# Attention and two expert layers on one core: engines of the moves chosen by a table, transposed probabilities in single banks, last keys of a pair in one operation

## The chip, the cores and the metric

The kernel runs on one core of a Trainium2 chip. The metric is the device time of one execution in microseconds (us). The core has five engines with a queue each: PE (TensorE, the matrix unit; its weight loads are shown apart as PEld), DVE (VectorE), ACT (ScalarE), POOL (GpSimd) and SP (SyncE, which here only starts transfers). SBUF is the memory that all of them work in; PSUM is the small memory of eight banks into which PE writes.

## The reference, cut to what matters

```python
def reference(q, k, v, moe, moe2):            # q, k, v: batch 2, 8 heads, 576 tokens, 64 columns
    q_rot, k_rot = rotate(q), rotate(k)       # x1*cos - x2*sin, x1*sin + x2*cos
    s = q_rot @ k_rot.T / 8
    p = exp(s - s.max(-1))
    p = p / (p.sum(-1) + 1e-09)
    x = (p @ v)                               # 1152 tokens x 512
    h = x @ moe.w_in                          # 512 x 2048
    x = (h * tanh(softplus(h))) @ moe.w_out   # 2048 x 512
    h = x @ moe2.w_in
    P = a[0] + a[1] * h + a[2] * h**2 + a[3] * h**3
    Q = 1.0 + abs(b[0]) * abs(h) + abs(b[1]) * h**2
    return (P / (Q + 1e-6)) @ moe2.w_out
```

All products are fp32. The kernel splits each factor into a high part that the fast product type takes and a low remainder, and adds three products: high by high, high by low, low by high. The four weight matrices arrive as 64-bit numbers, and their conversion to a high and a low part is work for ACT and DVE.

## The kernel before

**Stages.** The eight pairs of heads (four of batch 0, then four of batch 1) are the attention stage. The two expert layers follow, m = 0 (line 1034's `Mish`) and m = 1 (the `ratio` function), each in 12 steps: four chunks of 512 hidden columns by three blocks of 384 tokens. A step has two `up` operations of 24 products (L1012) and, a step later, three or four `down` operations of 12 products (L1096), whose sums are collected by `down.add` (L1100 copies the first chunk, L1102 adds the others).

**One pair of attention.** `turned` rotates q and k (`rope.1` to `rope.4`, L620 to L624; for the first keys L594 to L602). `columns` transposes them on PE (L643); ACT moves the high part out of PSUM (`turn.hi`, L658) and DVE the low part (`turn.lo`, L662). Scores come in five tiles (`score`, L719); the last 64 keys of a row are taken apart from the first 512 in `rests` (L690 on PE, `rest.move` L695 on ACT, `rest.max` L697 on DVE), once for tiles 0 and 1 and once for tiles 2 and 3. DVE scales a tile and takes its maximum (`score.max`, L734 and L754), ACT takes the exponential and its sum (`score.exp`, L738 and L759). `turn_p` transposes the probabilities (L786 to L796) into two neighbouring banks at a time, which are taken and given back together; `p.move` copies them to SBUF (L811), on ACT and DVE by turns. `weigh` multiplies by v (L845), and `weigh.move` copies the result (L850, ACT). `shares` turns the sums into factors: DVE adds 1e-9 and inverts (L865, L866, through a PSUM bank), PE transposes and spreads (L870, L878, L880), DVE scales (`x.scale`, L885), POOL splits into high and low (`x.hi` L896, `x.lo` L898).

**What sets the order.** Nothing in the program runs in the order in which it is written. `Plan.op` records every operation with an engine, an assumed cost, and what it reads and writes. `Plan.emit` then walks through time: it takes again and again the operation that could start first by these assumed costs, after a waiting penalty from the table `YIELD`, and breaks ties by a rank that the table `EARLY_LATE` shifts. It also hands out the PSUM banks. Operations named in `SHARED` (rotations, splits and the like, with their operands in SBUF) are not allowed to overlap one another in this walk, on whichever of DVE and POOL they are. The result is a fixed sequence for each engine; on the chip an engine does its sequence in order, and waits where an operand or a bank is not ready.

Of the kernel before, what the change touches and what calls it, by code (L numbers as in the profile page):

```python
# [44 lines left out]
def pool(n, wide=False):  # L45
# [13 lines left out]
    "down": -2293, "down.0": 1013, "down.add": -6295, "down.add.0": 4566, "g.hi": -9315, "g.hi.0": -1569, "g.lo":  # L59
# [51 lines left out]
YIELD = {  # L111
# [37 lines left out]
class Plan:  # L149
# [3 lines left out]
    def __init__(self):  # L153
# [56 lines left out]
    def emit(self, banks=8):  # L210
# [57 lines left out]
        while len(issued) < n:  # L268
# [24 lines left out]
            if names[i].removesuffix(".0") in SHARED:  # L293
                shared = end
# [902 lines left out]
```

## Time and profile before

| what | value |
|---|---|
| median of 3 runs | 539.42 us (539.36 to 539.58) |
| the profiled execution | 539.58 us, of which 537.7 us from its first to its last instruction |
| busy over the span | PE 97%, DVE 84%, ACT 68%, POOL 18% |
| granted TensorE clock | 1.00, which is the level of 2.4 GHz |
| first score, end of the last attention product, last expert product | 9.14 us, 139.45 us, 533.7 us |

A busy PE is not a PE at its best pace, since the ends of products are modelled and overlap. Whether it lost time is therefore read from the distance between the starts of two groups of products, compared with the same group elsewhere.

### The profile page before, as it was taken

How to read it: one execution, taken by the hardware profiler on the slowest of the kernel's cores; microseconds unless marked ns; L12 is line 12 of the kernel's file. 1: busy time of each engine (PE TensorE's matmuls, PEld its weight loads, DVE VectorE, ACT ScalarE, POOL GpSimd, SP SyncE). 2: the span in 40 equal slices, each digit the busy share in tenths (PEclk: the TensorE clock that was granted, in tenths of full speed). 3: DMA queues.
4: the chain of work that ended last, by engine and by line, in shares of the span. 5: the costliest groups of instructions: out<-in, count | busy, mean ns of one | idle time of the engine just before them, and what ended most of it. 6: DMA issues, size and time to landing. Idle time of an engine off the chain costs nothing.

```text
span 537.7 us, 9631 instructions
## 1 busy us (share of the span) xinstructions
PE 523.7 (97%) x3784; PEld 476.6 (89%) x3784; DVE 453.1 (84%) x704; ACT 367.5 (68%) x562; POOL 96.5 (18%) x100
## 2 busy tenths in 40 slices
PE   4999999999999999999999999999999999999997
PEld 3777777777999999999999999999889999889985
DVE  5789899998688959979788776999999898988892
ACT  3888889898786638697486667557677555676540
POOL 6899999212100000000000000000000000000000
PEclk9999999999999999999999999999999999999999
DMA  5433420033819494657639421044017003000022
GB/s 136 110 86 113 92 61 24 23 102 103 299 80 400 195 333 157 269 203 285 263 145 362 194 93 67 1 157 157 0 35 279 2 0 132 25 1 0 1 78 99
DMA packets 38684, 69.40 MB, mean 129 GB/s; under 512 B 22000, under 2 KB 24560, under 8 KB 37104
## 3 DMA queue, kind: packets, MB, share of 16 engines
q1 hardware_dynamic: 37824, 68.50, 35.5%
q8 instruction: 30, 0.49, 0.4%
q10 hardware_dynamic: 816, 0.30, 0.2%
q14 instruction: 14, 0.11, 0.1%
HBM read 53.84 MB, written 14.94 MB: 128 GB/s over the span
## 4 chain that ended last, share of the span: by engine, by line
PE 92%; ACT 4%; DVE 2%; issue 1%; DMA 0%; SPq 0%; DVEq 0%; ACTq 0%
PE banks L1012 37%; PE banks L1096 37%; PE banks L845 6%; PE banks L719 5%; PE banks L796 3%; PE banks L690 2%; ACT f L738 1%; ACT f L759 1%; PE banks L878 1%; PE banks L643 1%; ACT x L811 1%; DMA x<-in_k 0%; DVE f L594 0%; DVE x L811 0%; DVE f L754 0%
## 5 line engine op out<-in xcount | busy, mean ns | idle before, releaser
L1012 PE MATMUL banks<-r 128*128 128x384 f32 x1152 | 203.9, 335 | 0.0
L1096 PE MATMUL banks<-r 128*128 128x384 f32 (+1 forms) x1008 | 201.8, 358 | 0.0
L1012 PEld LDWEIGHTS banks<-r 128*128 128x128 f32 x1152 | 200.3, 188 | 0.9
L1096 PEld LDWEIGHTS banks<-r 128*128 128x128 f32 x1008 | 180.9, 188 | 16.4
L1022 ACT CAST r<-f 128x768 fp32r<-128x768 f32 x24 | 20.0, 833 | 40.8 <-DVE f L1070 40.8
L759 ACT ACTIVATE f<-f 128x576 f32<-128x576 f32 x56 | 43.1, 773 | 3.8 <-DVE f L754 3.7
L1034 ACT ACTIVATE r<-banks 128x768 fp32r<-128x768 f32 x24 | 19.6, 815 | 37.7 <-PE banks L1012 37.7
L845 PE MATMUL banks<-x,f 128*64 128x256 f32 (+1 forms) x320 | 42.4, 410 | 0.2
L719 PE MATMUL banks<-r 64*128 64x512 f32 (+2 forms) x264 | 39.9, 395 | 1.1 <-ACT r L658 0.5
L754 DVE TENSOR_SCALAR_CACHE_REDUCE f<-banks,f 128x512 f32<-128x512 f32 x56 | 38.8, 746 | 1.0
L1054 ACT ACTIVATE f<-banks 128x768 f32<-128x768 f32 x24 | 19.5, 812 | 25.9 <-PE banks L1012 25.9
L845 PEld LDWEIGHTS banks<-x,f 128*64 128x64 f32 x320 | 22.6, 136 | 14.8 <-DVE f L754 1.6
L1038 DVE TENSOR_TENSOR r<-f,r 128x768 fp32r<-128x768 f32 x24 | 22.8, 956 | 14.4 <-ACT f L1034 14.4
L1102 DVE TENSOR_TENSOR x<-banks,x 128x384 f32<-128x384 f32 (+1 forms) x42 | 25.0, 609 | 11.3 <-PE banks L1096 11.2
L1062 DVE TENSOR_TENSOR f<-f,banks 128x768 f32<-128x768 f32 x24 | 22.9, 953 | 13.2 <-ACT f L1060 13.0
L418 ACT ACT_TABLE_LOAD x26 | 33.4, 1283 | 0.5
L719 PEld LDWEIGHTS banks<-r 64*128 64x128 f32 (+1 forms) x264 | 27.7, 204 | 4.6 <-DVE r L662 0.8
L811 DVE COPY x<-banks 128x512 f32<-128x512 f32 (+2 forms) x52 | 28.4, 571 | 3.1 <-PE banks L796 2.0
L796 PEld LDWEIGHTS banks<-f 64*128 64x128 f32 x576 | 22.3, 141 | 5.6 <-ACT f L759 1.8
L811 ACT COPY x<-banks 128x512 f32<-128x512 f32 (+2 forms) x52 | 24.2, 495 | 4.3 <-PE banks L796 3.7
L796 PE MATMUL banks<-f 64*128 64x64 f32 x576 | 25.6, 230 | 0.8 <-DVE r L662 0.4
L1023 DVE TENSOR_TENSOR r<-f,r 128x768 fp32r<-128x768 f32 x24 | 22.9, 956 | 3.2 <-ACT r L1022 2.8
(95 smaller groups left out, 735.7 us busy)
## 6 DMA issues: line engine op xcount, KB each, us to landing
f<-in_moe_w_in SPq DMA_DIRECT2D x16, 1024.0 KB, 5.7
f<-in_moe_w_out SPq DMA_DIRECT2D x16, 1024.0 KB, 5.7
outside<-f SPq DMA_DIRECT2D x12, 1024.0 KB, 5.0
r<-outside SPq DMA_DIRECT2D x12, 1024.0 KB, 6.0
x<-in_k SPq DMA_DIRECT2D x15, 128.0 KB, 3.0
out<-x SPq DMA_DIRECT2D x5, 256.0 KB, 2.3
f<-in_q SPq DMA_DIRECT2D x8, 128.0 KB, 2.9
f<-in_v SPq DMA_DIRECT2D x8, 128.0 KB, 2.1
```

Of the source, the lines that this page charges most:

```text
L418: nc.scalar.preload_act_table_set(name)
L719: nc.tensor.matmul(o, qT[r, x, t * 128:(t + 1) * 128], kT[r, y, hf * w:(hf + 1) * w], start=(n == 0), stop=(n == 2))
L754: nc.vector.tensor_scalar(x[:, 0:8], bank(P).rearrange("p (k j) -> p k j", j=64), -0.125, nr, ALU.mult, ALU.min, accum_out=nm)
L759: nc.scalar.activation(view(at, 9, 64), x, AF.Exp, bias=nm, scale=-1.0, accum_out=sm)
L796: nc.tensor.transpose(bank(P)[:, hf, (i + n) * 64:(i + n + 1) * 64], x[r, f:f + 128], idf[r, r])
L811: (nc.scalar.copy if engine == "ACT" else nc.vector.tensor_copy)(o, i)
L845: nc.tensor.matmul(bank(P)[64 * a:64 * a + 64, 0:n], l, r, start=(kb == 0), stop=(kb == 4), skip_group_check=True)
L1012: nc.tensor.matmul(bank(P)[:, i, 0:BW], y[:, cb, f], x[:, cb, tok], start=(cb == 0 and n == 0), stop=(cb == CB - 1 and n == 2))
L1023: plan.op("g.lo", "DVE", dve(N), lambda: nc.vector.tensor_tensor(gl, g, gh.bitcast(F32), ALU.subtract), r=[(x,), (dst, u, "h")], w=[(dst, ...
L1062: plan.op("ratio.5", "DVE", dve(N, True), lambda: nc.vector.tensor_tensor(t, t, h(), ALU.mult), r=[(P,), (ba,)], w=[(bt,)])
L1096: nc.tensor.matmul(bank(P)[:, 0:n], x, y, start=(f == 0 and j == 0), stop=(f == FT - 1 and j == 2))
L1102: nc.vector.tensor_tensor(total(), bank(P)[:, 0:n], total(), ALU.add)
```

## The change

1. **A letter table.** `Plan.op` takes alternatives (`other`): the same work on another engine with another cost. A new table `ENGINES` says for each recorded operation which it is (A, D or P for ACT, DVE or POOL). It is open to `p.move`, `turn.hi`, `weigh.move`, `sum.row`, `rest.move` and the first `down.add` (ACT or DVE), the rotations, `x.lo`, `w.bound`, `w.lo` and `g.low` (POOL or DVE), and `x.hi` (POOL or ACT).
2. **Single banks.** The transposed probabilities of a full tile go into two banks that are taken and given back one by one.
3. **Last keys once.** `rests` does all four tiles of a pair in one product group of 24, one move of 512 columns and one maximum. The grid in SBUF has a tenth row for it.
4. **Sums.** ACT adds the 1e-9, and DVE inverts from SBUF to SBUF, so no bank is held for it.
5. **New tables.** `EARLY_LATE` and `YIELD` are new throughout, and so the whole sequence is another one.

```diff
 EARLY_LATE = {
-    "down": -2293, "down.0": 1013, "down.add": -6295, "down.add.0": 4566, "g.hi": -9315, "g.hi.0": -1569, "g.lo":
+    "down": 5156, "down.0": -6929, "down.add": -17362, "down.add.0": -2506, "down.add.0.ACT": 8843, "down.add.ACT":
...
+ENGINES = {
+    "down.add": "AAAADDDDDDDDDDDDDDDDDDDDDDDDDDDDDDDDDDDDDDDDDDAADDDADDDDDDDDDDDDDDDDDDDDDDDDD", "down.add.0":
+    "DADA", "g.low": "DPDDDDDDDPPPPPDPDDDDDP", "g.low.0": "PP", "p.move@0": "DADAAAAAAAA", "p.move@1":
...
-    def op(self, name, engine, cost, fn, r=(), w=(), late=0.0, after=(), form=None):
+    def op(self, name, engine, cost, fn, r=(), w=(), late=0.0, after=(), form=None, other=()):
         i = len(self.ops)
+        ways = [(engine, name, cost, fn)] + [(e, f"{name}.{e}", c, f) for e, c, f in other]
+        letter = ENGINES.get(name + at, "")[n:n + 1]
+        way = next((x for x in ways if x[0][0] == letter), ways[0])
+        engine, mark, cost, fn = way
...
-                    if names[i].removesuffix(".0") in SHARED:
+                    if names[i].removesuffix(".0") in SHARED and ops[i][0] in ("DVE", "POOL"):
                         t = max(t, shared)
...
-            for i in range(2):
-                t = 2 * u + i
+            for t in range(4):
                 for n, (x, y) in enumerate(((0, 0), (0, 1), (1, 0))):
                     for h, r in enumerate(HALVES):
-                        nc.tensor.matmul(bank(P)[:, h, i * 64:(i + 1) * 64], qT[r, x, t * 128:(t + 1) * 128],
+                        nc.tensor.matmul(bank(P)[:, h, t * 64:(t + 1) * 64], qT[r, x, t * 128:(t + 1) * 128],
                                          kT[r, y, 512:S], start=(n == 0), stop=(n == 2))
...
-        P = Banks(2)
+        P = [Banks(1), Banks(1)] if what == "m" and t < 4 else [Banks(2)]
...
-            T["moves"] = T.get("moves", 0) + 1
-            if T["moves"] % 2:
-                plan.op("p.move", "ACT", act(n), lambda hf=hf: move("ACT", hf), r=[(P,)], w=w)
-            else:
-                plan.op("p.move2", "DVE", dve(n, True) + (0 if n < 600 else 60), lambda hf=hf: move("DVE", hf), r=[(P,)], w=w)
+            ways = [("ACT", act(n), lambda hf=hf: move("ACT", hf)),
+                    ("DVE", dve(n, True) + (0 if n < 600 else 60), lambda hf=hf: move("DVE", hf))]
+            plan.op("p.move", *ways[0], r=[(P[hf],)], w=w, other=ways[1:])
...
-        def rec():
-            nc.vector.tensor_scalar_add(bank(P)[:, 0, 64:73], sm, 1e-9)
-            nc.vector.reciprocal(sm, bank(P)[:, 0, 64:73])
+        def some():
+            nc.scalar.activation(sm, sm, AF.Identity, bias=prm[:, 8:9], scale=1.0)
...
-        plan.op("sum.inv", "DVE", 340, rec, r=[], w=sums + [(P,)])
+        plan.op("sum.add", "ACT", 110, some, r=[("small",)], w=sums)
+        plan.op("sum.inv", "DVE", 220, lambda: nc.vector.reciprocal(sm, sm), w=sums)
```

Three places in the resulting sequences follow. The first is DVE at the very start, where the first keys are rotated; the lines 594 to 602 of before are 667 to 675 now, and 620 to 624 are all line 695. Before:

```order
L594 TENSOR_TENSOR f<-x,f 128x4x64 x4
L602 TENSOR_TENSOR x<-f 128x8x32
L600 TENSOR_TENSOR x<-f 128x8x32
L620 TENSOR_TENSOR f<-x,f 128x256
L621 TENSOR_TENSOR f<-x,f 128x256
L624 TENSOR_TENSOR x<-f 128x4x32
L622 TENSOR_TENSOR x<-f 128x4x32
```

Of the change:

```order
L695 TENSOR_TENSOR f<-x,f 128x128 x2
L667 TENSOR_TENSOR f<-x,f 128x4x64 x4
L695 TENSOR_TENSOR x<-f 128x2x32
L675 TENSOR_TENSOR x<-f 128x8x32
L673 TENSOR_TENSOR x<-f 128x8x32
L695 TENSOR_TENSOR x<-f 128x2x32
L695 TENSOR_TENSOR f<-x,f 128x256 x2
L695 TENSOR_TENSOR x<-f 128x4x32 x2
```

The four small rotations of the last keys (128x128 and 128x2x32), which POOL did beside DVE, are now in DVE's own sequence.

The second place is PE at the beginning of the second pair, with the last keys' products (L690, now L764) among transposes (L796, now L877) and scores (L719, now L798). Before:

```order
L796 MATMUL banks<-f 128x64 x16
L870 MATMUL banks<-f 9x64 x2
L796 MATMUL banks<-f 128x64 x4
L690 MATMUL banks<-r 128x64 x12
L719 MATMUL banks<-r 128x512 x12
L690 MATMUL banks<-r 128x64 x12
L719 MATMUL banks<-r 128x512 x6
```

Of the change:

```order
L877 MATMUL banks<-f 128x64 x32
L764 MATMUL banks<-r 128x64 x24
L877 MATMUL banks<-f 128x64 x4
L866 MATMUL banks<-f 128x64 x8
L868 MATMUL banks<-f 64x64
L869 MATMUL banks<-f 128x64
L798 MATMUL banks<-r 128x512 x18
```

Two groups of 12 became one of 24, and the scores behind it run 18 in a row.

The third place is POOL from the first expert step on, where before it had only `x.hi` and `x.lo` (L896, L898) left to do and then nothing. L553 is `w.bound`, L573 `w.lo`, L1124 `g.low`, L981 `x.lo`:

```order
L553 TENSOR_SCALAR f<-f 128x1024
L1124 TENSOR_TENSOR r<-f,r 128x768
L573 TENSOR_TENSOR r<-f,r 128x1024
L981 TENSOR_TENSOR r<-f,r 128x576
L553 TENSOR_SCALAR f<-f 128x1024
L1124 TENSOR_TENSOR r<-f,r 128x768
L553 TENSOR_SCALAR x<-x 128x1024
L1124 TENSOR_TENSOR r<-f,r 128x768
```

POOL goes on like this through the whole first layer: 10 `g.low` in all, and of `w.bound` and `w.lo` 12 and 18 in the program.

## Rows read from the trace of the kernel before

**Rows 1.** The page: span, and PE's busy time with its share.

```profile
span 537.7 us, 9631 instructions
PE 523.7 (97%) x3784; PEld 476.6 (89%) x3784; DVE 453.1 (84%) x704; ACT 367.5 (68%) x562; POOL 96.5 (18%) x100
```

**Rows 2.** The chain that ended last, expert stages: start us, length us, what.

```profile
139.52 12.70 PE banks L1012 x72
...
509.21 24.54 PE banks L1096 x108
533.77 0.69 DVE x L1102
```

**Rows 3.** Stretches: length, then busy PE, PEld, DVE, ACT, POOL, then clock, DMA.

```profile
10.00:130.00 120.00, 117.59 (x1553) 90.79 (x1553) 108.06 (x272) 102.05 (x263) 86.22 (x77) 1.00 0.29 74
139.50:347.50 208.00, 208.00 (x1201) 208.00 (x1201) 167.48 (x212) 143.97 (x155) 2.58 (x2) 1.00 0.54 210
```

**Rows 4.** The chain that ended last, attention: one good example of each group.

```profile
77.50 0.76 PE banks L719 x6
...
107.03 1.14 PE banks L796 x36
108.16 0.72 PE banks L690 x12
108.89 1.44 PE banks L719 x12
111.05 2.31 PE banks L845 x20
...
119.38 2.84 PE banks L845 x20
...
131.89 4.38 PE banks L1012 x24
```

**Rows 5.** PE in order of time, 60 to 70 us: start us, length us, what.

```profile
61.60 0.53 PE L643 MATMUL banks<-f,x 64*128 64x64 f32 x11
62.18 2.91 PE L845 MATMUL banks<-x,f 128*64 128x320 f32 x20
...
66.87 0.64 PE L878 MATMUL banks<-r 64*128 64x128 f32 x4
...
67.63 1.05 PE L719 MATMUL banks<-r 128*128 128x288 f32 x6
68.62 0.46 PE L643 MATMUL banks<-f 64*128 64x64 f32 x8
```

**Rows 6.** PE in order of time, elsewhere in attention.

```profile
9.14 3.25 PE L719 MATMUL banks<-r 64*128 64x288 f32 x24 [0.47 <-ACT r L658]
...
33.20 1.39 PE L643 MATMUL banks<-f,x 64*128 64x64 f32 x11
34.81 1.95 PE L719 MATMUL banks<-r 64*128 64x512 f32 x12 [0.22 <-DVE x L811]
...
92.25 1.56 PE L796 MATMUL banks<-f 64*128 64x64 f32 x36
93.86 2.69 PE L719 MATMUL banks<-r 128*128 128x288 f32 x18
```

**Rows 7.** All engines in order of time, the start.

```profile
4.18 0.64 POOL L621 TENSOR_TENSOR f<-x,f 128x128 f32<-128x128 f32 x1
3.92 2.09 DVE L594 TENSOR_TENSOR f<-x,f 128x256 f32<-128x256 f32 x4 [2.95 <-DMA x<-in_k]
6.85 0.42 DVE L620 TENSOR_TENSOR f<-x,f 128x256 f32<-128x256 f32 x1
```

**Rows 8.** In order of time: one POOL operation, and one DVE operation twice.

```profile
90.71 1.56 POOL L621 TENSOR_TENSOR f<-x,f 128x640 f32<-128x640 f32 x1
...
91.21 1.61 DVE L481 TENSOR_SCALAR f<-f 128x1024 f32<-128x1024 f32 x1
...
120.59 0.69 DVE L481 TENSOR_SCALAR f<-f 128x1024 f32<-128x1024 f32 x1
```

More of the change, by code (lines that the diff above doesn't have):

```diff
@@ new lines @@
+    "turn.lo@q.b": 12835, "turn@1": 4247, "turn@2": -6983, "turn@3": 1832, "turn@4": 16692, "turn@5": 2447,
+    "turn@6": 918, "turn@7": 8261, "turn@k.e": 13147, "turn@k.m": 11567, "turn@q.a": 11603, "turn@q.b": 9487, "up":
[15 rows of a table added]
+    "y.hi": 9962, "y.lo": -22857}
+YIELD = {
+    "down": 91, "down.0": 304, "down.add": 1093, "down.add.0": 187, "down.add.0.ACT": 610, "g.hi": 191, "g.lo": 576,
[22 rows of a table added]
+    "turn@k.m": 777, "turn@q.b": 90, "up.0": 576, "w.bound": 1037, "w.bound.0.POOL": 1769, "w.bound.POOL": 1164,
+    "w.hi": 365, "w.hi.0": 343, "w.keep": 1251, "w.lo.0.POOL": 1005, "w.lo.POOL": 234, "w.load": 508, "w.load.0":
[8 rows of a table added]
@@ L135 @@
+ENGINES = {
+    "down.add": "AAAADDDDDDDDDDDDDDDDDDDDDDDDDDDDDDDDDDDDDDDDDDAADDDADDDDDDDDDDDDDDDDDDDDDDDDDDDD", "down.add.0":
[13 rows of a table added]
+    "AAA", "turn.hi@4": "DAD", "turn.hi@5": "ADD", "turn.hi@6": "ADA", "turn.hi@7": "ADA", "turn.hi@k.e": "A",
+    "turn.hi@k.m": "A", "turn.hi@q.a": "A", "turn.hi@q.b": "A", "w.bound": "DPDDPDDDPDPDDPDDPPDDDDPDDDDD",
[5 rows of a table added]
 class Buf:
@@ L160, in __init__ @@
         self.names = []
+        self.keys = []
+        self.ways = []
+        self.count = {}
         self.wait = []
@@ L171, in ring @@
         return Buf(off + n * (i % size), n)
-    def op(self, name, engine, cost, fn, r=(), w=(), late=0.0, after=(), form=None):
+    def op(self, name, engine, cost, fn, r=(), w=(), late=0.0, after=(), form=None, other=()):
         i = len(self.ops)
+        at = "" if self.group is None else f"@{self.group}"
+        n = self.count[name + at] = self.count.get(name + at, -1) + 1
+        ways = [(engine, name, cost, fn)] + [(e, f"{name}.{e}", c, f) for e, c, f in other]
+        letter = ENGINES.get(name + at, "")[n:n + 1]
+        way = next((x for x in ways if x[0][0] == letter), ways[0])
+        engine, mark, cost, fn = way
+        self.keys.append(mark + at)
+        self.ways.append((name + at, [(e, k + at, c) for e, k, c, _ in ways], ways.index(way)))
         deps, order = set(), set(after)
@@ L200, in op @@
         deps.discard(i)
-        key = name if self.group is None else f"{name}@{self.group}"
-        self.rank.append(i + EARLY_LATE.get(key, EARLY_LATE.get(name, 0)))
-        self.wait.append(YIELD.get(key, YIELD.get(name, 0)))
+        self.rank.append(i + EARLY_LATE.get(mark + at, EARLY_LATE.get(mark, 0)))
+        self.wait.append(YIELD.get(mark + at, YIELD.get(mark, 0)))
         self.names.append(name)
@@ L292, in emit @@
             issued.append(i)
-            if names[i].removesuffix(".0") in SHARED:
+            if names[i].removesuffix(".0") in SHARED and ops[i][0] in ("DVE", "POOL"):
                 shared = end
@@ L497, in hi, with rest @@
                 nc.scalar.copy(two()[0], whole(raw, n))
-            def rest(raw=raw, n=n, two=two):
+            def rest(raw=raw, n=n, two=two, eng=nc.vector):
                 wh, wl = two()
-                nc.vector.tensor_tensor(wl, whole(raw, n), wh.bitcast(F32), ALU.subtract)
+                eng.tensor_tensor(wl, whole(raw, n), wh.bitcast(F32), ALU.subtract)
             if wide:
                 val = vals[n]
-                plan.op("w.bound" + z, "DVE", 640, bound, w=[val])
+                plan.op("w.bound" + z, "DVE", 640, bound, w=[val], other=[("POOL", pool(1024, True), lambda f=bound: f(eng=nc.gpsimd))])
                 plan.op("w.shift" + z, "DVE", 640, shift, w=[val])
@@ L510, in prepare @@
             plan.op("w.hi" + z, "ACT", act(1024, False), hi, r=[src], w=[kh])
-            plan.op("w.lo" + z, "DVE", dve(1024), rest, r=[src, kh], w=[kl])
+            plan.op("w.lo" + z, "DVE", dve(1024), rest, r=[src, kh], w=[kl],
+                    other=[("POOL", pool(1024), lambda f=rest: f(eng=nc.gpsimd))])
             if way == "keep":
@@ L605, in turned @@
     def turned(p, n, engine, ts=slice(0, 5), at=None):
-        eng = {"DVE": nc.vector, "POOL": nc.gpsimd}[engine]
-        cost = dve if engine == "DVE" else pool
         m = ts.stop - ts.start
@@ L669, in columns @@
         plan.op("turn", "PE", 60 * len(rows) + 20, pe, r=src + [("idf",)], w=[(P,)], form="rows")
-        plan.op("turn.hi", "ACT", act(n[0]) + 200 * (n[1] - 1), hi, r=[(P,)], w=kh)
+        plan.op("turn.hi", "ACT", act(n[0]) + 200 * (n[1] - 1), hi, r=[(P,)], w=kh,
+                other=[("DVE", dve(n[0], True) + 150 * (n[1] - 1), lambda: hi(nc.vector.tensor_copy))])
         plan.op("turn.lo", "DVE", dve(n[0], True) + 150 * (n[1] - 1), lo, r=[(P,), *kh], w=kl)
@@ L685, in pe, with src @@
         def pe():
-            for i in range(2):
-                t = 2 * u + i
+            for t in range(4):
                 for n, (x, y) in enumerate(((0, 0), (0, 1), (1, 0))):
                     for h, r in enumerate(HALVES):
-                        nc.tensor.matmul(bank(P)[:, h, i * 64:(i + 1) * 64], qT[r, x, t * 128:(t + 1) * 128],
+                        nc.tensor.matmul(bank(P)[:, h, t * 64:(t + 1) * 64], qT[r, x, t * 128:(t + 1) * 128],
                                          kT[r, y, 512:S], start=(n == 0), stop=(n == 2))
-        nm, x = view(T["nm", p].off + 16 + 4 * u, 4), grid[:, 8]
-        plan.op("rest", "PE", 590, pe, r=[(bq, u, z) for z in "hl"] + [(bk, "e", z) for z in "hl"], w=[(P,)], form="rows", late=90)
-        plan.op("rest.move", "ACT", act(256), lambda: nc.scalar.mul(
-            x.rearrange("p (h m) -> p h m", h=2), bank(P)[:, :, 0:128], -0.125), r=[(P,)], w=[(gr, "r")])
-        plan.op("rest.max", "DVE", dve(256), lambda: nc.vector.tensor_reduce(
-            nm, x.rearrange("p (h j) -> p h j", j=64), axis=AX.X, op=ALU.min), r=[(gr, "r")], w=[(T["nm", p], "r", u)])
+        nm, x = view(T["nm", p].off + 16, 8), grid[:, 8:10].rearrange("p u (h m) -> p u h m", h=2)
+        plan.op("rest", "PE", 1180, pe, r=[(bq, u, z) for u in range(2) for z in "hl"] + [(bk, "e", z) for z in "hl"], w=[(P,)],
+                form="rows", late=90)
+        def src():
+            return bank(P)[:, :, 0:256].rearrange("p h (u m) -> p u h m", u=2)
+        plan.op("rest.move", "ACT", act(512), lambda: nc.scalar.mul(x, src(), -0.125), r=[(P,)],
+                other=[("DVE", dve(512, True), lambda: nc.vector.tensor_scalar(x, src(), -0.125, None, ALU.mult))], w=[(gr, "r", u, h, z) for u in range(2) for h in range(2) for z in range(2)])
+        plan.op("rest.max", "DVE", dve(512), lambda: nc.vector.tensor_reduce(
+            nm, grid[:, 8:10].rearrange("p u (k j) -> p (u k) j", j=64), axis=AX.X, op=ALU.min),
+            r=[(gr, "r", u, h, z) for u in range(2) for h in range(2) for z in range(2)], w=[(T["nm", p], "r")])
     def score(p, t):
@@ L759, in exp @@
             nc.scalar.activation(view(at, 9, 64), x, AF.Exp, bias=nm, scale=-1.0, accum_out=sm)
-        plan.op("score.max", "DVE", 671, most, r=[(P,), (T["nm", p], "r", t // 2)], w=[(T["nm", p], i), k])
-        plan.op("score.exp", "ACT", act(576, False, 2), exp, r=[(T["nm", p], i), k, (gr, "r")], w=[(e, h), (T["sm", p], i)], form="exp")
+        plan.op("score.max", "DVE", 671, most, r=[(P,), (T["nm", p], "r")], w=[(T["nm", p], i), *k])
+        plan.op("score.exp", "ACT", act(576, False, 2), exp, r=[(T["nm", p], i), k[0], (gr, "r", u, h, t % 2)], w=[(e, h), (T["sm", p], i)], form="exp")
     def places(p):
@@ L814, in turn_p @@
         n = 256 if what == "r" else 512 if t < 4 else 1000
-        plan.op("p.turn", "PE", 140 if what == "r" else 500 if t < 4 else 330, pe, r=r + [("idf",)], w=[(P,)], form="rows")
+        plan.op("p.turn", "PE", 140 if what == "r" else 500 if t < 4 else 330, pe, r=r + [("idf",)], w=[(x,) for x in P], form="rows")
         for hf in range(2 if what == "m" and t < 4 else 1):
@@ L850, in weigh @@
         plan.op("weigh.move", "ACT", act(n), lambda: nc.scalar.copy(view(XF, S)[:, c], bank(P)[:, 0:n]),
+                other=[("DVE", dve(n, True), lambda: nc.vector.tensor_copy(view(XF, S)[:, c], bank(P)[:, 0:n]))],
                 r=[(P,)], w=[(bf, hf)])
@@ L896, in shares, with low @@
         plan.op("x.hi", "POOL", pool(576, True), lambda: nc.gpsimd.tensor_tensor(
-            xh[:, j, d], xf, tiny[:, 1:2].to_broadcast([128, S]), ALU.mult), r=parts, w=[("xh", b, j)])
-        plan.op("x.lo", "POOL", pool(576), lambda: nc.gpsimd.tensor_tensor(
-            xl[:, j, d], xf, xh[:, j, d].bitcast(F32), ALU.subtract), r=parts + [("xh", b, j)], w=[("xl", b, j)])
+            xh[:, j, d], xf, tiny[:, 1:2].to_broadcast([128, S]), ALU.mult), r=parts, w=[("xh", b, j)],
+                other=[("ACT", act(576, False), lambda: nc.scalar.copy(xh[:, j, d], xf))])
+        def low(eng):
+            eng.tensor_tensor(xl[:, j, d], xf, xh[:, j, d].bitcast(F32), ALU.subtract)
+        plan.op("x.lo", "POOL", pool(576), lambda: low(nc.gpsimd), r=parts + [("xh", b, j)], w=[("xl", b, j)],
+                other=[("DVE", dve(576), lambda: low(nc.vector))])
     LAG = 2
@@ L1037, in mish, with low @@
         plan.op("g.hi" + first, "ACT", act(N), lambda: f(gh), r=[(P,)], w=[(dst, u, "h")], form="mish")
-        plan.op("g.low" + first, "DVE", dve(N), lambda: nc.vector.tensor_tensor(gl, w, gh.bitcast(F32), ALU.subtract),
-                r=[(bw,), (dst, u, "h")], w=[(dst, u, "l")])
+        def low(eng):
+            eng.tensor_tensor(gl, w, gh.bitcast(F32), ALU.subtract)
+        plan.op("g.low" + first, "DVE", dve(N), lambda: low(nc.vector), r=[(bw,), (dst, u, "h")], w=[(dst, u, "l")],
+                other=[("POOL", pool(N), lambda: low(nc.gpsimd))])
     def ratio(P):
@@ L1114, in down @@
         plan.op("down" + ".0" * (s == 0), "PE", 12 * (173.5 if m == 0 else 227), pe, r=src, w=[(P,)])
-        plan.op("down.add" + ".0" * (s == 0), "DVE", dve(n, True), add, r=[(P,)], w=[(A,)])
+        plan.op("down.add" + ".0" * (s == 0), "DVE", dve(n, True), add, r=[(P,)], w=[(A,)],
+                other=[("ACT", act(n), lambda: add(nc.scalar.copy))] * (c == 0))
         if c == NCH - 1 and m == 0:
```

76 lines of the change are left out of this document (39 added, 37 removed), and 172 rows, old and new, of tables (EARLY_LATE, ENGINES, YIELD).

## The prediction

> **What bounds the kernel now.** I read the page first: of a span of 537.7 us PE is busy for 523.7 [rows 1]. The profiled execution took 539.58 us, so 1.88 lie outside the span, and it stands 0.16 above the median of 539.42; the sum is made against 539.58 and then taken down by 0.16. A busy PE says little by itself, so the next view is the chain that ended last. From 139.52 on it is one unbroken row of expert products: 72 of 384 columns in 12.70 us, which is 0.176 each, and so on until 509.21 + 24.54 = 533.75, where one DVE addition and the store end it [rows 2]. In the stretch of the first layer PE is busy for 208.00 of 208.00 us at clock 1.00, which is the level of 2.4 GHz [rows 3]. So 394 us of the span are a sequence that nothing in this change makes shorter; it can only be broken. What can become shorter lies before 139.5.
>
> There PE is the bound as well, but with gaps. In the 120 us from 10 to 130 PE is busy for 117.59, DVE for 108.06, ACT for 102.05, POOL for 86.22 [rows 3]. 2.4 us of open idleness understate the loss. I therefore compare each group with a good example of its kind, from start to start. Per program: 8 weighings of 256 and 8 of 320 columns at 2.31 and 2.84 (41.2 us), 14 times 12 scores of 512 columns at 1.44 (20.2), 656 transposes of probabilities at 1.14 for 36 (20.8), 14 groups of last keys at 0.72 (10.1) [rows 4]; 139 transposes of q and k after the first 13 at 0.58 for 11 (7.3), 8 spreads at 67.63 - 66.87 = 0.76 (6.1), 16 groups of six 288-column scores at 68.62 - 67.63 = 0.99 (15.8) [rows 5]. That is 121.5 us. The stretch from the first score at 9.14 [rows 6] to 139.52 [rows 2], less one expert group of 4.38 put in ahead [rows 4], is 126.0. So about 4.5 us are waits that a better order could take away, and 9.14 us at the head are a chain of their own.
>
> **The change part by part.**
>
> *Start.* Before, DVE's first four rotations of 256 columns took 2.09 us while POOL rotated the last keys beside it; alone such a rotation takes 0.42 [rows 7]. Four at 0.42 are 1.68, so POOL's company cost 0.41, or more where neighbours overlap. Now DVE also does the last keys' four small operations, and POOL is silent. At 256 columns 0.42; I take 0.2 for each small one, an estimate between nothing and 0.42. That is 0.8 more on DVE and at least 0.4 less, and two of the four can start before the main keys have landed. POOL's chain for them began only at about the same time, so nothing is waiting longer for the tables. Bounds: 4 x 0.42 - 0.41 = 1.3 late, and 0.6 early if all four hide. I take 0.2 early: PE's first product also waited for POOL's last small rotation, and that goes. The score at 9.14 starts near 8.9.
>
> *Banks and engines of the moves.* The clearest loss is at 33.20: 11 transposes of new q and k take 34.81 - 33.20 = 1.61 us, where the same 11 take 0.58 at 61.60 [rows 5, 6]. The group behind it names DVE's copy as what it waited for, that is, a bank not yet emptied. Another is at 92.25, where 36 transposes take 1.61 instead of 1.14 [rows 4, 6]. These two hold 1.03 + 0.47 = 1.5 of the 4.5 us. Single banks attack the first kind: a bank whose copy is done is free although its neighbour's is not. The free choice of engine attacks the second: a copy need not queue on DVE because its turn came. The work itself is no smaller. DVE loses 12 full copies of probabilities, 8 small additions, some of the conversion of the weights, and gains 12 rotations, 7 `turn.hi`, 7 `weigh.move`; ACT gains 12 copies, 5 `x.hi` and 8 additions, and loses what DVE gained. By count DVE comes out even and ACT a little fuller, on a stretch where ACT had 18 of 120 us free and DVE 12 [rows 3]. So this is a better fit, not a lighter load. Bounds: nothing, and all of the 4.5. I take 1.5, a third: the two losses that I can name, or their like.
>
> *Last keys in one operation.* Seven pairs lose one change of group on PE. Two groups of six scores cost 2 x 0.76 = 1.52, one of twelve 1.44 [rows 4], so a join is worth 0.08, and seven 0.56. Against it stands that the products now need all of q and not half, and that the maximum of tile 0 waits for the last keys of tile 3, some 0.72 us of PE longer [rows 4]; the scores queue behind that maximum on DVE, and ACT's exponentials behind them. With scores enough in the banks this is hidden. Bounds: 0.6 gained, 7 x 0.72 = 5 lost if every pair waited. I take 0.5 gained, since the sequence puts other transposes beside the group.
>
> *Sums.* The addition moves to ACT, eight times, and lengthens the chain from the last exponential to the spread by one hop. PE does transposes and scores meanwhile; only for the last pair is there less to do, and there the 72 expert products of which the first 24 need no new tokens (4.38) stand behind it [rows 2, 4]. Nothing, and 0.5 if that cover were gone.
>
> *Expert layers.* POOL takes 8 `w.bound`, 15 `w.lo` and 10 `g.low` after the first chunk. A two-input operation of 640 columns takes POOL 1.56 [rows 8], so by proportion 2.5 at 1024 and 1.9 at 768. The nearest consumer is `down`, which needs `g.low`; but a step's products separate them (48 products, 8.4 us by the 0.176 of rows 2), against 1.9 for the split on POOL and two operations of ACT ahead of it. The weights have a whole chunk of time. DVE had 40 us free in those 208 [rows 3] and gets freer. I take nothing, with 5 us as a bound if some splits come late. The second layer has no POOL work and the same operations; its order on DVE is new, and I take nothing there either.
>
> The sum: 539.58 - 0.2 - 1.5 - 0.5 = 537.4, and 537.2 against the median of runs.
>
> **The rivals.**
>
> *Nearly all of the 4.5 is found.* The old sequence lost most in its first pairs, where POOL's rotations and DVE's copies were late together, and precisely these get choices. Then 539.4 - 4.5 - 0.2 - 0.5 = 534.2. Against it: the old order had been fitted to the same durations, and every shift opens some new wait.
>
> *Nothing comes of it.* The waits that go return elsewhere, because PE's neighbours are as busy as before. Then the time is that of before, 538.5 to 540.3.
>
> *POOL holds DVE up.* Where: in attention, at the rotations and `x.lo` that now run on DVE between maxima, while POOL rotates. At 91.21 a `w.bound` on DVE took 1.61 us, at 120.59 the same took 0.69; the slow one began when POOL's operation of 1.56 us from 90.71 was under way, and ended 0.55 after it [rows 8]. It was held for 0.92. DVE gets 12 rotations and 2 `x.lo` of that kind after the start. Held for 0.92 each they cost 12.9 us, against 11.9 that DVE has free between 10 and 130 [rows 3]. It decides from about 0.4 each: below, the 6 us lie in free time, above, maxima come late, then exponentials, then PE's transposes. At 0.92 perhaps a third reaches PE, 4 us, and with 0.7 gained at start and joins the time would be 542.7. For it: the sequence of an engine is fixed, and nothing on the chip keeps the two apart. Against it: the walk does keep `SHARED` operations apart, and PE paces both.
>
> The Trainium skill (SBUF — State Buffer, "Who interferes with whom") states this as a rule: the pair of ports that DVE shares with GpSimd is an exclusive lock, taken also by a DVE operation with two SBUF inputs against a GpSimd operation that reads SBUF, and whichever starts second waits for the whole of the other. By that rule, the first layer would be in question too; the trace agrees for the one `w.bound` at 91.21, and shows no two-input case as plainly beyond the slow start.
>
> What complete exclusion would mean there can be worked out from rows: DVE's 167.5 us, less at least 33 x 0.69 that leave it, plus 8 x 2.5 + 15 x 2.5 + 10 x 1.9 = 76 on POOL are 221 us in 208 [rows 3, 8]. That would make the layer up to 13 us longer, if nothing overlapped; but additions of PSUM sums and ACT's work fill such gaps, so I give it no case of its own beyond this rival.
>
> **How the numbers follow.** About 0.2% or 1.1 us is what a measurement can tell from no change. The forecast's own range is 535.5 to 538.3, with a chance of 0.53; nearly all found 0.17; nothing 0.16; POOL holds DVE 0.14. Faster is the first two, 0.70; same 0.16; slower 0.14. The range for 8 in 10 leaves out a little of the second below and the third rival above: 533.4 to 540.3.
>
> **What would show it.** The first score near 8.9 instead of 9.14. The expert products begin their unbroken row near 137 instead of 139.5, and end as much earlier; their pitch stays at 0.176. No group of 11 transposes takes 1.6 us. On PE no wait for `g.low` or `w.lo` between 140 and 350. DVE's rotations of 640 columns are short (some 0.8 us); if they take 1.5 and more, the third rival is at work. The prediction is wrong if the row begins near 139.5 or later, or if it is broken in the first layer.

## The result, and the profile after

The changed kernel takes 542.75 us (median of 6 runs, 540.98 to 544.68), the kernel before beside it 539.42 (6 runs, 539.25 to 539.79): a ratio of 1.0065, 95% interval 1.0042 to 1.0088. It is slower by 3.3 us, outside my range and on the other side. The profiled execution took 544.22 us, 1.5 above the median of its kernel, so single places below add up to more than 3.3.

The page of the changed kernel, answering to [rows 1]:

```profile
span 542.0 us, 9651 instructions
PE 523.8 (97%) x3784; PEld 477.3 (88%) x3784; DVE 449.5 (83%) x666; ACT 370.2 (68%) x571; POOL 180.8 (33%) x112
```

PE does what it did before, in 4.3 us more of span. POOL's busy time has nearly doubled, from 96.5 to 180.8; DVE's went down by only 3.6.

The same stretches as in [rows 3], the second from where the row of expert products now begins (length; busy PE, PEld, DVE, ACT, POOL; clock; DMA):

```profile
10.00:130.00 120.00, 116.13 (x1517) 91.94 (x1515) 110.50 (x269) 108.01 (x260) 87.59 (x62) 1.00 0.33 90
140.70:348.70 208.00, 206.73 (x1192) 206.41 (x1192) 155.72 (x166) 135.36 (x150) 86.27 (x32) 1.00 0.56 210
```

Two losses: PE is a little less busy in attention, and in the expert stretch it is no longer busy all the time. The clock is the same. The first score and the beginning of the row, PE in order of time, and then the end of the chain, answering to [rows 2, 6]:

```profile
9.01 3.25 PE L798 MATMUL banks<-r 64*128 64x288 f32 x24 [0.47 <-ACT r L732]
...
140.66 1.51 PE L1097 MATMUL banks<-r 128*128 128x384 f32 x7
```

```profile
513.48 24.54 PE banks L1184 x108
538.02 0.02 issue
538.04 0.69 DVE x L1190
```

The start came as forecast (9.01 for "near 8.9"). The row begins at 140.66, in the chain of waits at 140.73 where before it was 139.52 [rows 2]: 1.2 us later, not 2.5 earlier. Its last piece begins at 513.48 instead of 509.21 [rows 2]: 4.3 later, so 3.1 are lost inside the row. From product to product the row of before loses 0.1 us in all beyond its pitch, this one 3.25, nearly all of it in two places, near 336 and near 370 us.

Four of these bounds stand ahead of the row, and one place where the row is made late is in the timeline of 114 to 119 us (L553 is `w.bound`):

```profile
114.56 3.63 POOL L553 TENSOR_SCALAR f<-f 128x1024 f32<-128x1024 f32 x1 [2.63 <-ACT f L538]
...
118.22 0.69 DVE L556 TENSOR_SCALAR f<-f 128x1024 int32<-128x1024 int32 x1 [1.49 <-POOL f L553]
...
118.83 0.21 DVE L967 RECIPROCAL f<-f 128x9 f32<-128x9 f32 x1
...
119.09 0.23 PE L949 MATMUL banks<-f 64*9 64x64 f32 x2 [0.82 <-DVE f L967]
```

POOL's `w.bound` takes 3.63 us. DVE's `w.shift` (L556) waits for it, and DVE works in order: the reciprocal of a finished pair (L967), which needs no weights at all, stands behind it, and PE waits for that, 0.82 us here. All calls of that line, minimum, median and maximum in ns:

```profile
L553 DVE TENSOR_SCALAR x<-x x14: 682/688/957, 150.4 to 321.3; 128x1024 f32<-128x1024 f32 x14
L553 POOL TENSOR_SCALAR f<-f x6: 3622/3626/3988, 64.2 to 260.2; 128x1024 f32<-128x1024 f32 x6
L553 POOL TENSOR_SCALAR x<-x x6: 3628/3828/4475, 149.4 to 323.7; 128x1024 f32<-128x1024 f32 x6
...
who waited for it (us, times):
DVE f L556: 8.1, 5
```

Four of the twelve lie in attention, eight in the first expert layer. My price was 2.5 us; the program's own cost is `100 + 1.82 * 1024` ns = 1.96.

The breaks in the row, by the chain of waits before the first of them:

```profile
322.03 2.26 DVE x L556
...
324.32 1.95 DVE x L559
...
326.35 1.06 ACT f L569
...
327.43 1.24 DVE f L573
...
328.68 5.14 DMA outside<-f
...
333.91 1.88 ACT f L1148 x2
335.79 1.64 ACT f L1152 x2
```

Here the last weight half that is kept for the second layer is shifted, split and stored (L556 to L573, then the DMA; its bound was DVE's own, at 321.31), and ACT's `ratio.4` (L1148) waits for the end of that store: the ratio's buffers lie over the raw weights. Two of these steps on DVE are long: L556 takes 2.25 us where 0.69 is usual, and `w.low` (L559) 1.94 instead of 1.22. So is the `y.lo` (L1208) ahead of them, 2.45 instead of 0.55. Each lies beside an operation of POOL, L559 beside a bound of 4.07 us from 323.70, the other two beside splits:

```profile
317.24 2.41 POOL L573 TENSOR_TENSOR f<-x,f 128x1024 fp32r<-128x1024 f32 x1 [10.08 <-ACT f L569]
317.61 2.45 DVE L1208 TENSOR_TENSOR r<-f,r 128x384 fp32r<-128x384 f32 x1 [0.65 <-ACT r L1206]
...
321.89 1.84 POOL L1124 TENSOR_TENSOR r<-f,r 128x768 fp32r<-128x768 f32 x1 [2.24 <-ACT r L1119]
322.03 2.25 DVE L556 TENSOR_SCALAR x<-x 128x1024 int32<-128x1024 int32 x1
```

The wait list names who is late next:

```profile
PE banks L1097 <- DVE f L1151: 1.3, 1, 1.3
PE banks L1184 <- DVE f L1151: 1.3, 1, 1.3
```

`ratio.6` (L1151) frees the banks of a product; it comes late twice.

### The profile page after: what moved, and what is told of

Read it like the earlier page. It is cut to its first block, busy times and chain, and to the rows that moved or that the text cites. A ratio compares the mean times of both kernels' runs of the same rounds, so it can differ in the third digit from the quotient of the medians.

```text
span 542.0 us, 9651 instructions
## 1 busy us (share of the span) xinstructions
PE 523.8 (97%) x3784; PEld 477.3 (88%) x3784; DVE 449.5 (83%) x666; ACT 370.2 (68%) x571; POOL 180.8 (33%) x112
## 4 chain that ended last, share of the span: by engine, by line
PE 65%; DVE 15%; ACT 9%; POOL 4%; issue 2%; DMA 2%; ACTq 0%; SPq 0%; POOLq 0%
PE banks L1184 24%; PE banks L1097 24%; PE banks L924 6%; PE banks L798 5%; PE banks L877 3%; DVE x L559 3%; POOL f L553 2%; DVE r L1124 1%; DVE x L556 1%; DVE r L1208 1%; PE banks L764 1%; DVE x L1190 1%; ACT L490 1%; POOL f L695 1%; DVE x L553 1%
## 5 line engine op out<-in xcount | busy, mean ns | idle before, releaser
L798 PE MATMUL banks<-r 64*128 64x512 f32 (+2 forms) x264 | 40.3, 397 | 1.1 <-ACT r L732 1.1
L892 ACT COPY x<-banks 128x512 f32<-128x512 f32 (+2 forms) x71 | 31.2, 491 | 2.9 <-PE banks L877 2.0
L1119 ACT ACTIVATE f<-banks 128x768 f32<-128x768 f32 x24 | 19.5, 812 | 19.5 <-PE banks L1097 19.3
L798 PEld LDWEIGHTS banks<-r 64*128 64x128 f32 (+1 forms) x264 | 29.0, 207 | 3.9 <-ACT r L732 1.4
L1152 ACT ACTIVATE f<-f 128x768 f32<-128x768 f32 x24 | 22.3, 933 | 12.5 <-DVE f L1147 12.5
L1124 DVE TENSOR_TENSOR r<-f,r 128x768 fp32r<-128x768 f32 x14 | 19.4, 1388 | 12.9 <-ACT r L1119 12.8
L559 DVE SCALAR_TENSOR_TENSOR x<-f,x 128x1024 int32<-128x1024 int32 x20 | 29.5, 1474 | 0.7
L553 POOL TENSOR_SCALAR x<-x 128x1024 f32<-128x1024 f32 x6 | 23.4, 3910 | 18.4 <-ACT x L538 18.4
L1142 ACT ACTIVATE f<-banks 128x768 f32<-128x768 f32 x24 | 19.3, 805 | 13.9 <-PE banks L1097 13.9
L1124 POOL TENSOR_TENSOR r<-f,r 128x768 fp32r<-128x768 f32 x10 | 20.0, 2001 | 26.0 <-ACT r L1119 17.8
L1148 ACT ACTIVATE f<-banks,f 128x768 f32<-128x768 f32 x24 | 23.7, 990 | 6.7 <-PE banks L1097 4.7
```

Source lines behind the costliest of these rows:

```text
L553: eng.tensor_scalar(whole(raw, n), whole(raw, n), -WORD_MOST * WORD_SIGN, WORD_MOST, ALU.max, ALU.min)
L559: nc.vector.scalar_tensor_tensor(cut(n), words(raw, 0), 29, cut(n), ALU.logical_shift_right, ALU.bitwise_or)
L798: nc.tensor.matmul(o, qT[r, x, t * 128:(t + 1) * 128], kT[r, y, hf * w:(hf + 1) * w], start=(n == 0), stop=(n == 2))
L892: (nc.scalar.copy if engine == "ACT" else nc.vector.tensor_copy)(o, i)
L1124: eng.tensor_tensor(gl, w, gh.bitcast(F32), ALU.subtract)
```

## The experiments

In e1 to e4 and e6 the walk that sets the order is the changed kernel's, and only the engine on which an operation is issued differs, at the same place (the diff is cut at `...`; e5, e8 and e10 also move some operations in the finished order):

```diff
+FORCE = {'w.bound': 'D', 'w.bound.0': 'D'}
 ...
         self.ways.append((name + at, [(e, k + at, c) for e, k, c, _ in ways], ways.index(way)))
+        fn = next((x[3] for x in ways if x[0][0] == FORCE.get(name)), fn)
```

Theory A: POOL's `w.bound`, longer than planned, holds DVE's queue up. Rival B: the two-input operations on POOL do. Rival C: the new order in attention is itself worse, above all its rotations on DVE.

Times beside the kernel before in the same call; the last two columns are from the profiled execution, breaks being what the row loses beyond its pitch:

| kernel | us | before, us | ratio, 95% interval | row begins | breaks |
|---|---|---|---|---|---|
| the change | 542.75 | 539.42 | 1.0065, 1.0042 to 1.0088 | 140.66 | 3.25 |
| e1_bound_dve | 539.75 | 539.53 | 1.0003, 0.9994 to 1.0011 | 137.21 | 1.95 |
| e2_splits_dve | 545.08 | 539.53 | 1.0100, 1.0086 to 1.0115 | 143.49 | 1.66 |
| e3_all_dve | 542.97 | 539.53 | 1.0063, 1.0051 to 1.0075 | 141.51 | 1.62 |
| e4_ropes_pool | 544.03 | 539.53 | 1.0084, 1.0054 to 1.0114 | 140.48 | 3.21 |
| e5_keep_early | 539.24 | 539.91 | 0.9994, 0.9985 to 1.0003 | 138.30 | 1.73 |
| e6_bound_first_four | 540.86 | 539.91 | 1.0024, 1.0014 to 1.0033 | 138.64 | 3.23 |
| e7_before_bounds | 543.01 | 539.91 | 1.0063, 1.0050 to 1.0075 | 141.51 | 1.38 |
| e8_change_free | 540.38 | 539.72 | 1.0016, 1.0007 to 1.0025 | 137.70 | 2.55 |
| e9_bound_one_op | 539.69 | 539.72 | 1.0003, 0.9995 to 1.0012 | 138.43 | 1.97 |
| e10_store_first | 538.16 | 539.65 | 0.9967, 0.9954 to 0.9980 | 138.21 | 0.11 |

**e1_bound_dve**, the diff above: the 12 bounds on DVE.

> The changed kernel with its sequence of operations kept, but the 12 w.bound that POOL does are done by DVE at the same place of the walk. Theory A (POOL's w.bound is the cause: it takes 3.6 us and more where the walk assumed 1.96, and DVE's w.shift, which comes next in DVE's fixed sequence, waits for it with everything behind it): both breaks of PE near 336 and 371 us vanish, the wait of 0.8 us near 118 us vanishes, the expert row begins near 139.5, and the median falls from 542.75 to about 539.3. Rival B (POOL's two-input splits w.lo and g.low, which hold DVE off their shared port): little changes, 542 or more. Rival C (the attention sequence itself, rotations on DVE): the breaks near 336 and 371 vanish, the expert row still begins near 140.7, 540.7.

Almost the whole loss is gone, 539.75, the time that A gives; but it is made up otherwise than I said. The row begins at 137.21 instead of near 139.5, and 1.95 us of breaks stay that were to vanish. A holds for the bounds and leaves a second cause. C falls: without the bounds on POOL the row begins earlier than in the kernel before (139.45 by the same count).

**e2_splits_dve**, **e3_all_dve**: the splits on DVE, with the bounds left on POOL, and with them.

```diff
+FORCE = {'w.lo': 'D', 'w.lo.0': 'D', 'g.low': 'D', 'g.low.0': 'D'}
 ...
+FORCE = {'w.bound': 'D', 'w.bound.0': 'D', 'w.lo': 'D', 'w.lo.0': 'D', 'g.low': 'D', 'g.low.0': 'D'}
```

> The changed kernel with its sequence kept, but the 18 w.lo and 10 g.low that POOL does are done by DVE; the 12 w.bound stay on POOL. Theory A: the breaks of PE shrink a little at most, since w.bound still takes 3.6 us and holds w.shift up; 541.5 to 543. Rival B: the breaks vanish and the median is 540.5 or less.

> The changed kernel with its sequence kept, and all 40 of w.bound, w.lo and g.low on DVE, as in the kernel before. Both A and B: PE unbroken from the begin of the expert row, near 539.3. If attention itself is better in the new order (my prediction), 537.5; if the new attention order is worse without POOL's w.bound too (C), 540.5.

Both are slower than with the splits on POOL, by 2.3 (545.08 against 542.75) and by 3.2 us (542.97 against e1), and both lie outside every case that I had set. The second difference is the one to read, since the profiles of e1 and e3 have the full clock throughout: with the bounds on DVE, the splits are better on POOL, because DVE is too full when it does them. In e3's wait list PE waits for a maximum (L838):

```profile
PE banks L928 <- DVE f L838: 1.3, 2, 1.2
```

e2 can't be read so. In its profile, and in e4's, the granted clock falls near 120 us; in all the others it is 1.00 until the last product has ended. The stretch from 120 to 130 us, e2 and then e4 (columns as in [rows 3]):

```profile
120.00:130.00 10.00, 10.00 (x74) 7.83 (x74) 9.08 (x21) 7.34 (x14) 1.42 (x1) 0.66 0.33 107
...
120.00:130.00 10.00, 10.00 (x99) 7.27 (x97) 8.31 (x22) 7.63 (x19) 3.84 (x3) 0.83 0.24 99
```

A mean of 0.66 between the levels of 2.4 and 1.2 GHz is 6.8 us at the lower one. The same 30 scores take 6.44 us in e2 and 4.06 in e3:

```profile
122.27 6.44 PE L802 MATMUL banks<-r 128*128 128x288 f32 x30
...
120.95 4.06 PE L802 MATMUL banks<-r 128*128 128x288 f32 x30 [0.42 <-DVE f L778]
```

At half pace 6.8 us cost at most 3.4, an estimate from the two levels; without them e2 would stand near 541.7, not above the change. In the 10 us ahead of it PE was busy for 8.46. That does not explain it, for in e3 PE was busy for only 8.41 of the ten from 120 on, and the clock stayed; the cause is open. So B is not refuted by e2. Against B as the whole cause stand e1 and e9, which keep the splits on POOL and lose nearly nothing. For a part of it stands the row: its breaks shrink to 1.66 in e2, as far as in e1, where I had said "a little at most".

**e4_ropes_pool**: rotations and `x.lo` of the pairs 1 to 7 back on POOL; the table is looked up by name and pair.

```diff
+FORCE = {f"rope.{i}@{p}": "P" for i in range(1, 5) for p in range(1, 8)} | {"x.lo@6": "P", "x.lo@7": "P"}
```

> The changed kernel with its sequence kept, but the 12 rotations and 2 x.lo of pairs 1 to 7 that DVE does go to POOL. My third rival (POOL holds DVE up at rotations in attention) says that this wins back the loss in attention, 1.2 us, so that the expert row begins near 139.5. Theory A: no gain there; POOL has 12 x 1 us more to do than planned and the row begins at 141 or later, 543 or more.

544.03, no better in the median, but this decides nothing: the clock in the profile of e4 is at the lower level for 3.4 us (0.83 in the row under e2), worth up to 1.7, more than the 1.2 in question. Its runs go from 540.28 at a mean clock of 0.997 to 547.28 at 0.990. What speaks on the third rival is the length of the rotations themselves, further down.

**e6_bound_first_four**: only the four bounds of attention on DVE.

```diff
+FORCE = {'w.bound.0': 'D'}
```

> The changed kernel, in which of the 12 bounds on GpSimd only the four that lie in the attention stage go back to VectorE; the eight of the first expert layer stay on GpSimd. It splits the 3.0 us that e1 gave back. If the four alone cost it: row of the expert layers at about 137.2, time about 540 to 540.5. If the eight in the row do (through held VectorE work that makes the layer change late): row at 140.5, time 542 to 543. By the breaks of the changed kernel and of e1 (3.25 and 1.95 us) I expect 1.3 us from the eight and the rest from the four: 540.5 to 541.

540.86, 0.9 us above the kernel before in its call. The four gave back 2.4 of the 3.3 us, the eight of the row hold 0.7 more (e1 stands 0.2 above). The breaks are the changed kernel's, 3.2.

**e7_before_bounds**: the kernel before with the same 12 bounds on POOL.

```diff
-                plan.op("w.bound" + z, "DVE", 640, bound, w=[val])
+                k = plan.turns["bound" + z] = plan.turns.get("bound" + z, -1) + 1
+                eng = nc.gpsimd if z or "DPDDPDDDPDPDDPDDPPDDDDPDDDDD"[k] == "P" else nc.vector
+                plan.op("w.bound" + z, "DVE", 640, lambda f=bound, e=eng: f(eng=e), w=[val])
```

> The kernel before, its order untouched, with the same 12 bounds of the words (four in attention, eight in the first expert layer) on GpSimd instead of VectorE: this part of the change alone. If a bound on GpSimd takes 3.6 us and VectorE waits behind it: slower, 541.5 to 543, most of it as a later beginning of the row of the expert layers (140.5 to 142 instead of 139.5). If the bounds only hurt together with the new order: within 0.3 us of 539.5.

543.01: this part alone costs 3.1 us in the old order as well. Its timeline shows the step in the row to which I had given no price:

```profile
146.58 3.63 POOL L481 TENSOR_SCALAR f<-f 128x1024 f32<-128x1024 f32 x1 [0.48 <-ACT f L466]
...
150.24 0.69 DVE L484 TENSOR_SCALAR f<-f 128x1024 int32<-128x1024 int32 x1 [6.88 <-POOL f L481]
...
154.45 1.82 DVE L1040 TENSOR_TENSOR r<-f,r 128x768 fp32r<-128x768 f32 x2
155.46 0.79 PE L1098 MATMUL banks<-r 128*128 128x384 f32 x3 [1.00 <-DVE r L1040]
```

DVE stands still for 6.88 us until the bound is done, `g.low` (L1040) is behind it in DVE's queue, and `down` (L1098) waits. Some 3.1 of the 6.88 pass before ACT's L466 has made the bound's input, and such a wait stands in the kernel before too; there DVE does the bound itself in 1.03 us:

```profile
142.68 1.03 DVE L481 TENSOR_SCALAR f<-f 128x1024 f32<-128x1024 f32 x1 [2.27 <-ACT f L466]
```

**e9_bound_one_op**: the changed kernel, POOL's bound with one comparison.

```diff
-                eng.tensor_scalar(whole(raw, n), whole(raw, n), -WORD_MOST * WORD_SIGN, WORD_MOST, ALU.max, ALU.min)
+                if eng is nc.vector:
+                    eng.tensor_scalar(whole(raw, n), whole(raw, n), -WORD_MOST * WORD_SIGN, WORD_MOST, ALU.max, ALU.min)
+                else:
+                    eng.tensor_scalar(whole(raw, n), whole(raw, n), WORD_MOST, None, ALU.min)
```

> The changed kernel with its 12 bounds on GpSimd, each with one comparison instead of two (the lower bound is left out there; VectorE's 20 keep both). If the long time of the operation is what costs (Theory A): should an operation with one comparison take some 1.9 us instead of 3.62, as the program's cost table has it, about half of the 3.0 us that e1 gave back comes back, 540.8 to 541.5; if it takes 3.6 us as well, nothing changes, 542.5 to 543. If the place on GpSimd costs and not the length (a wait on another engine and back): 542.5 to 543 even at 1.9 us.

The operation takes 2.77 us instead of 3.62, not the 1.96 of the program's cost:

```profile
L556 POOL TENSOR_SCALAR f<-f x6: 2766/2770/2787, 63.9 to 257.9; 128x1024 f32<-128x1024 f32 x6
```

And the time is 539.69, where e1 stands: 0.85 us off each of twelve is worth all of the 3 us. So it is the length that costs, not the change of engine. I had expected about half.

**e5_keep_early**: e1, with the six steps of the last kept weight half (bound to store) each right behind that of the half before.

```diff
+        last = max(i for i in issued if names[i] == "w.keep")
+        for i in range(last - 5, last + 1):
+            issued.remove(i)
+            issued.insert(issued.index(i - 6) + 1, i)
         for i in issued:
             ops[i][2]()
```

> The changed kernel with all bounds of the words on VectorE (as in e1, 539.75 us), and one thing more: the six steps of the last weight half that is kept for the second expert layer (bound, shift, low, high copy, split, store) stand right behind the same steps of the half before it, instead of some 9 us later. In e1 the row of the expert layers begins at 137.2 us and loses 1.95 us in breaks at the change from the first layer to the second, where ScalarE waits for that store. Theory (the late store holds up the first ratios, and these the banks): the breaks fall under 0.5 us and the time to about 538.2 (537.8 to 538.7). Rival (VectorE is late there with its own work, whatever the store does): the breaks stay between 1.5 and 2 us and the time at 539.5 to 540.

539.24, between the two. The breaks near 333 and 366 are gone, so the store did cause them. A new one of 1.5 us stands at 318 to 320, because DVE's moved work is now ahead of a `down.add` and a `y.lo` that PE needs:

```profile
319.94 0.44 PE L1105 MATMUL banks<-r 128*128 128x384 f32 x1 [0.93 <-ACT r L1214]
```

**e8_change_free**: e1, with bound, shift and low of the last half (1126 to 1128) behind that `y.lo`, and the `w.lo` of the half before (1124, moved with them) and one `g.low` (1116) from POOL to DVE.

```diff
+FORCE = {'w.bound': 'D', 'w.bound.0': 'D', 1116: 'D', 1124: 'D'}
 ...
+        behind = max(i for i in issued if names[i] == "y.lo" and i < 1120)
+        for i in (1124, 1126, 1127, 1128):
+            issued.remove(i)
+            issued.insert(issued.index(behind) + 1, i)
+            behind = i
```

> The kernel of e1 (all bounds on VectorE, 539.75 us), with the layer change cleared by other means than in e5: the last weight half's bound, shift and low stand behind the last y.lo of their step instead of in front of it, and two operations that lie there on GpSimd (a split of weights and one of the middle values), in whose time VectorE's y.lo and low took 2.45 and 2.75 us instead of 0.56 and 1.22, are on VectorE. In e5 the breaks at the ratios were gone but one of 1.5 us stood at 318 us, where a y.lo came late. Theory (store and y.lo in time leave no break): breaks under 0.5 us, time 538.2 (537.6 to 538.7), better than both kernels. Rival (VectorE has no room there, the work only changes its place): breaks of 1.5 us or more again, 539.2 to 539.8.

540.38, a miss: 0.7 us above before. DVE is in time now, and its `y.lo` there takes 0.56 us, but the store is not. SyncE's DMA issues, and the step of the chain:

```profile
316.12 2.02 SPq L516 DMA_DIRECT2D r<-outside  x2
321.15 0.35 SPq L595 DMA_DIRECT2D outside<-f  x1
```

```profile
321.15 9.02 DMA outside<-f
...
330.26 1.88 ACT f L1157 x2
```

The store of 1 MB leaves at 321.15 instead of e1's 323.78, and lands at 330.2 instead of 329.1: two loads of 1 MB each were issued ahead of it. The Trainium skill (DMA: Bandwidth & Descriptors, "Queues, rings and completion order") says that each DMA engine consumes the descriptors of a ring in order; the trace agrees, 9.0 us behind two loads against 5.3 in e1, where they had a head start of 8 us.

**e10_store_first**: e8, and this store ahead of those two loads, which fetch weights of the second layer.

```diff
+        for i in (1177, 1176):
+            issued.remove(i)
+            issued.insert(issued.index(1131) + 1, i)
```

> The kernel of e8 (540.38 us) with one thing more: SyncE issues the store of the last weight half ahead of two loads of 1 MB for the second expert layer instead of behind them. In e8 the store was issued 2.6 us earlier than in e1 (321.15 against 323.78 us), and landed later (9.0 us after its issue instead of 5.3, at 330.2), since the loads, issued at 316.1, filled the queue (1 MB takes 4.8 us alone). If the store's landing is what holds the ratios up: it lands at about 326.5, the first break (0.76 us at 333) goes, the second (1.46 at 367) shrinks under 0.7, time 538.6 to 539.2. If VectorE's own load at the layer change makes the breaks: they stay at 1.5 us or more together, 539.8 to 540.5.

538.16 us, ratio 0.9967 (0.9954 to 0.9980): 0.3% below the kernel before, and 0.4 us below what I expected. The store now leaves at 321.67 and takes 4.7 us. In its chain the row has no break where there were two:

```profile
325.69 16.64 PE banks L1196 x96
342.33 16.64 PE banks L1109 x96
358.97 8.20 PE banks L1196 x36
367.17 4.88 PE banks L1109 x28
```

## Why the prediction was wrong

**The step that failed** is *Expert layers*: "I take nothing, with 5 us as a bound if some splits come late". In place of nothing the runs show 3.1 us for the bounds on POOL and 1.7 for the change of layers. It failed in four ways.

1. *The price.* I took a two-input operation of 640 columns in proportion, 2.5 us at 1024. For the two-input splits `w.lo` (L573) and `g.low` (L1124) that held, with medians of 2.40 and 1.86:

```profile
L573 POOL TENSOR_TENSOR r<-f,r x8: 2377/2402/3118, 83.9 to 340.8; 128x1024 fp32r<-128x1024 f32 x8
```

```profile
L1124 POOL TENSOR_TENSOR r<-f,r x10: 1843/1864/2652, 119.9 to 321.9; 128x768 fp32r<-128x768 f32 x10
```

   `w.bound` is another form, one input and two comparisons, and takes 3.62. e9 shows that the excess decides: at 2.77, near my price, nothing is lost against DVE. The next two points say where the excess lands; at 2.77 they cost nothing.
2. *The count.* I spoke of eight bounds after the first chunk. The four ahead of it, in attention, are the larger loss (2.4 of 3.1 us by e6, as medians of runs that scatter by a microsecond and more), and they stand in no term of my sum.
3. *Who stands behind it.* "The weights have a whole chunk of time" is true of the weights. But DVE's `w.shift` follows the bound, and all that DVE has queued behind it waits too: a reciprocal at 118.83, `g.low` in e7. "DVE had 40 us free" is no cover for that.
4. *The second layer.* "Its order on DVE is new, and I take nothing there either." The last two kept halves went to their stores between 302.67 and 306.10 in the old order, the last one at 328.68 in the new. The runs price that: with the bounds on DVE the time stands 0.2 above before, and with a free layer change 1.5 below, so 1.7 us. Three things went together there: the order of the steps, the place of the store behind two loads, and DVE held beside POOL's splits (2.45 and 2.25 us where 0.55 and 0.69 are usual). What each is worth alone was not measured; the place of the store is 2.2 us, once the other two are done (e8 against e10).

**The terms that held** are those of attention, smaller than said. With both causes removed (e10) the kernel gains 1.5 us where the sum said 2.2, just inside the forecast's own range, and the row begins at 138.21 where I had said near 137. The score begins at 9.01 for 8.9. That the single banks, the engines of the moves and the joined last keys each bring what I gave them was not separated; only their sum was measured.

So the 5.5 us between forecast and result are 3.1 for the bounds (3.3 less e1's 0.2), 1.7 for the layer change and 0.7 for a gain in attention that was too large. These are differences of medians; the changed kernel's alone is known to about 1.2 us either way (1.0042 to 1.0088).

**The rivals.** POOL did hold DVE up, as the third one said, and that its 542.7 is the time that came is a coincidence: its 4 us were to be lost at the rotations. There DVE's five of 640 columns took 0.76 to 0.82 us and its seven of 320 columns 0.48 to 1.39. Against the shortest of each kind that is 0.18 us in the mean, an estimate, where this rival needed 0.4. The holding that I had there in mind exists in the first layer. `w.low` (two inputs), minimum, median and maximum, after; before, its maximum was 1.226:

```profile
L559 DVE SCALAR_TENSOR_TENSOR x<-f,x x20: 1224/1226/3382, 151.8 to 332.7; 128x1024 int32<-128x1024 int32 x20
```

The Trainium skill (SBUF — State Buffer, "Who interferes with whom") has DVE operations with two SBUF inputs and GpSimd's reads exclude each other; these maxima agree. Such holding took part in the late store at the change of layers. It is not the larger cause, since e1 and e9 leave every split on POOL and stand at the time of before; and the layer did not become 13 us longer, as complete exclusion would have it: the whole row lost 3.1.

## What to carry to other kernels

An operation on another engine is priced by a row of its own form, with its number of comparisons, not by a neighbour's time per column; where no row has it, its price is open to both sides, and a planner that takes it too short can put the next engine's whole queue behind it. Where an order is new, look in every layer for the last transfer that a reused buffer waits for, and in its queue for what was issued ahead of it: an earlier issue can land later. An engine's free time in a stretch hides nothing if what it waits for is at the head of its queue. And before two times are compared, look at the clock of both: e2 and e4 seemed to answer a question that they left open.

## What the runs showed of the hardware that I had not expected

- On POOL a `tensor_scalar` of 128 x 1024 float32 takes 3.62 us with two comparisons and 2.77 with one; a two-input operation of that size 2.40. DVE does the first in 0.69.
- One execution of a fixed order differs in attention by a microsecond: e1, e5, e8 and e10 have the same order there, and their rows begin at 137.21, 138.30, 137.70 and 138.21. The changed kernel's runs lie 3.7 us apart, those of before in the same call 0.5. Where a part is priced from one profile, that is the error to keep in mind.
- The granted clock can fall in one order and not in its neighbour: for 6.8 us near 120 us in e2's profile, with a mean clock of 0.994 to 0.996 in all four of its runs, and not in e3's, where PE had a stretch of ten that was as empty (8.41 us busy).
